# A one-token decoder block on one core: slots of 65,280 bytes a row, the last values in one transfer, a shared tile, 16 output rows

## The chip, the cores and the metric

The kernel runs on one core of one Trainium2 chip. The metric is device time in microseconds (us) of one execution; lower is better. The kernel before took 1052.56 us as the median of three runs (1052.41, 1052.56, 1052.56).

## The reference

One token passes through a transformer block with an adaptive layer norm. All data are float32. What is computed, cut to what matters:

```python
mod = (silu(c) @ w_mod).reshape(1, 6, 1, -1)          # six rows of 640: sa, ca, ga, sb, cb, gb
h = layernorm(x) * (1 + ca) + sa
q = (h @ wq).reshape(32 heads, 192)
p = softmax((q @ k_cache) * 192 ** -0.5)              # k_cache: 32 heads x 8192 positions x 192
o = p @ v_cache                                       # v_cache: 32 heads x 8192 positions x 192
x = x + ga * (o.reshape(6144) @ wo)
h = layernorm(x) * (1 + cb) + sb
x = x + gb * (relu(h @ w1 + b1) ** 2 @ w2 + b2)       # 640 -> 1536 -> 640
```

The two caches are 201 MB each and are read once; with the weights the kernel reads 451.83 MB.

## The kernel before, in words

**The stream.** The host lays out the caches, `wo` and most of `wq` as one array `kv`. `plan()` (line 55) cuts it into 53 chunks. A chunk has, for each of the 128 partitions, one contiguous row: `nk` key positions of 192 floats, then `nv` value blocks of `UNIT` = 1536 floats (8 positions), then perhaps one part of `wo` (1920 floats, "o") and one of `wq` (2560 floats, "q"). A chunk is filled up to `SLOT` = 84 x 192 = 16128 floats, that is 64,512 bytes a row. Three buffers of that size (`slot`, line 102) take the chunks in turn. `load(n)` (line 227) issues chunk `n` on SP's DMA queue, and the loop over the plan calls `load(n + 3)` at the end of chunk `n`'s step; SP holds the load back until the last instruction that reads the buffer's old contents is done. After the 53 chunks the same three buffers take, in this order, `wm1` (12800 floats a row, in two transfers), `w1` (7680, in two) and `w2` (7680, in four), so `wm1` waits for chunk 50, `w1` for chunk 51 and `w2` for chunk 52. All go through one queue, in the order of their issue.

**A chunk's step** (lines 377 to 424). `query` multiplies a part of `wq` on TensorE, and ScalarE puts the result in the ring `qb` (line 248, 1536 floats). `values` (line 314) does three products per value block, which the profile counts as six TensorE instructions, all of them for the heads whose probabilities are ready. `multiply` (line 267) multiplies keys by the query on VectorE; GpSimd folds 7 of 16 positions in half (line 399), and VectorE sums (`scores`, line 276). When a head's 64 positions are complete, `softmax` (line 292) makes its probabilities, with a transpose on TensorE in the middle. A head whose eight value blocks are done is evicted in the next step: `evict` (line 327) masks and reduces on VectorE, and for each second head transposes on TensorE; `turn` (line 342) reduces that on VectorE. `attend` (line 347) multiplies a pair of heads by its part of `wo`: ScalarE spreads the vector, then eight TensorE instructions add to `att_a`.

**The end** (lines 431 to 469). The last head is evicted (line 334, 336), transposed (340), turned (344) and attended (352 to 356). Then 40 TensorE instructions on `wm1` make three modulation rows (line 198). Between them `gather` (line 361) brings the attention's sum from PSUM to `att_s` (a tile of 640 floats, zeroed by GpSimd at line 260, near the program's start) and adds its parts on TensorE (line 369). Second layer norm, `w1` (line 447), two matmuls on `ones` that compute nothing (line 451), the squared ReLU, `w2` (line 464, 96 TensorE instructions), two VectorE instructions (467, 468) and the store (469) of four rows of 160 floats, taken from partitions 0, 32, 64 and 96.

**The last three chunks** by `plan()`: chunk 50 has 42 key positions, the last ones, and 5 value blocks; chunk 51 has no keys, 9 value blocks and o 14; chunk 52 has 7 value blocks and o 15, 12672 floats. Chunk 52 alone is loaded in two transfers (line 231): four value blocks first, the rest behind them.

## Time and profile before

| | |
|---|---|
| Runs shown | 1052.41, 1052.56, 1052.56 us |
| The profiled execution's own time | 1052.4 us |
| Its span, from the first to the last instruction | 1050.6 us |
| TensorE busy | 486.7 us (46%) |
| VectorE busy | 826.2 us (79%) |
| ScalarE busy | 44.9 us (4%) |
| GpSimd busy | 190.5 us (18%) |
| Mean granted TensorE clock | 0.729 |
| Bytes read | 451.83 MB |

The profile names engines PE (TensorE matmuls), PEld (TensorE weight loads), DVE (VectorE), ACT (ScalarE), POOL (GpSimd) and SPq (the queue on which SP issues DMAs). Times in a view are microseconds from the start of the span. In the chain of waits, each row is a start, a duration and what ran; the chain is followed back from the last instruction to what released it. In a timeline, the brackets at a row's end hold how long the engine stood idle before it and what it waited for. In a table of stretches, each row has a stretch, its length, busy time and instructions of each engine, the granted clock, the DMA engines' busy share and the rate in GB/s.

### The profile page before, as it was taken

Reading aid. Unit: us, or ns where it says so; the run is one execution under the profiler, and the core shown is the slowest. Engines: PE = TensorE matmul, PEld = TensorE weight load, DVE = VectorE, ACT = ScalarE, POOL = GpSimd, SP = SyncE. Lnnn points to the kernel's source line nnn. Section 1 sums busy time; section 2 is a strip of 40 time slices with the busy share of each in tenths; the row PEclk is TensorE's granted clock in tenths of the full one; section 3 lists DMA queues with packets and bytes.
Section 4 is the critical chain, followed back from the end, with each engine's and each line's share of the span. In section 5 each row is a group of like instructions: output and inputs, shape, how many; then the busy total and the mean of one; then the engine's idle time right before and its main releaser. Section 6 shows DMA issues by size and latency. Waiting matters only on the chain.

```text
span 1050.6 us, 5178 instructions
## 1 busy us (share of the span) xinstructions
PE 486.7 (46%) x2130; PEld 133.8 (13%) x2130; DVE 826.2 (79%) x405; ACT 44.9 (4%) x122; POOL 190.5 (18%) x61
## 2 busy tenths in 40 slices
PE   3253334455352363436353356345446346435287
PEld 1010001111010010101011011001001011001023
DVE  1799878876959969888697895999887977988812
ACT  0100000000000000000000000000000000000001
POOL 1113121121212211212121121122211211211200
PEclk9676576777675686767677687686777767768689
DMA  9999999999999999999999999999999999999997
GB/s 406 432 433 432 431 440 442 436 436 430 433 432 432 435 440 433 432 429 434 432 433 435 435 431 434 432 438 432 438 437 431 432 430 430 432 435 440 420 432 336
DMA packets 9142, 452.14 MB, mean 430 GB/s; under 512 B 1032, under 2 KB 1036, under 8 KB 1420
## 3 DMA queue, kind: packets, MB, share of 16 engines
q1 hardware_dynamic: 9120, 451.83, 99.4%
q8 instruction: 16, 0.26, 0.1%
q14 instruction: 6, 0.05, 0.0%
HBM read 451.83 MB, written 0.00 MB: 430 GB/s over the span
## 4 chain that ended last, share of the span: by engine, by line
DMA 56%; DVE 30%; PE 12%; ACT 1%; issue 0%; SPq 0%; DVEq 0%; ACTq 0%
DMA chunk<-in_kv 53%; DVE chunk L273 16%; DVE sc L281 12%; PE ps_o L322 6%; PE ps_q L254 2%; PE att_a L354 2%; DMA w_t<-in_w 2%; DMA wm_t<-in_wm 1%; DVE os L336 1%; DVE om L334 1%; PE att_a L356 0%; ACT p L305 0%; PE ps_mx L297 0%; PE ps_mod L198 0%; PE ps_mod L204 0%
## 5 line engine op out<-in xcount | busy, mean ns | idle before, releaser
L273 DVE TENSOR_TENSOR chunk<-chunk,qb 128x8064 f32<-128x8064 f32 (+19 forms) x81 | 419.6, 5211 | 126.7 <-DMA chunk<-in_kv 121.5
L281 DVE TENSOR_REDUCE sc<-chunk 128x25 f32<-128x4800 f32 (+21 forms) x109 | 333.8, 3096 | 0.4
L399 POOL TENSOR_TENSOR chunk<-chunk 128x1824 f32<-128x1824 f32 (+9 forms) x51 | 187.4, 3675 | 801.3 <-DVE chunk L273 552.2
L322 PE MATMUL ps_o<-chunk,p 128*32 128x512 f32 x1536 | 287.1, 716 | 68.8 <-DMA chunk<-in_kv 59.4
L297 PE MATMUL ps_mx<-ident,mp 128*128 128x128 f32 x32 | 14.6, 457 | 350.4 <-DVE mp L295 350.4
L322 PEld LDWEIGHTS ps_o<-chunk,p 128*32 128x32 f32 x1536 | 66.0, 128 | 265.1 <-issue 181.4
L354 PE MATMUL att_a<-chunk,oW 128*32 128x512 f32 x96 | 64.2, 824 | 44.9 <-ACT oW L352 44.9
L254 PE MATMUL ps_q<-chunk,ln_h 128*128 128x512 f32 x110 | 66.4, 764 | 25.9 <-DMA chunk<-in_kv 25.9
L297 PEld LDWEIGHTS ps_mx<-ident,mp 128*128 128x128 f32 x32 | 5.7, 177 | 379.5 <-DVE mp L295 310.8
L305 ACT ACTIVATE p<-sc,nm 128x256 f32<-128x256 f32 x32 | 16.2, 508 | 650.2 <-DVE nm L299 650.2
L254 PEld LDWEIGHTS ps_q<-chunk,ln_h 128*128 128x128 f32 x110 | 26.4, 251 | 63.6 <-issue 34.4
L334 DVE TENSOR_TENSOR om<-ps_o,mask 96x512 f32<-96x512 f32 x32 | 21.6, 675 | 8.9 <-PE ps_o L322 8.9
L299 DVE TENSOR_REDUCE nm<-ps_mx 128x1 f32<-128x128 f32 x32 | 9.3, 292 | 19.4 <-PE ps_mx L297 19.4
L336 DVE TENSOR_REDUCE os<-om 96x64 f32<-96x512 f32 x32 | 21.8, 682 | 1.1
L354 PEld LDWEIGHTS att_a<-chunk,oW 128*32 128x32 f32 x96 | 12.1, 141 | 81.3 <-ACT oW L352 47.6
L344 DVE TENSOR_REDUCE oT<-ps_oT 128x3 f32<-128x96 f32 x16 | 4.0, 248 | 20.9 <-PE ps_oT L340 20.9
L310 PE MATMUL ps_sum<-ident,wide 128*128 128x128 f32 x16 | 7.4, 466 | 22.4 <-ACT wide L308 22.4
L340 PE MATMUL ps_oT<-ident,os 96*128 96x96 f32 x16 | 5.0, 314 | 27.0 <-DVE os L336 27.0
L198 PE MATMUL ps_mod<-wm_t,silu 128*32 128x480 f32 (+2 forms) x78 | 9.0, 602 | 14.4 <-DVE silu L180 14.4
L356 PE MATMUL att_a<-chunk,oW 128*96 128x384 f32 x32 | 14.5, 534 | 0.0
L352 ACT ACTIVATE oW<-oT,r 128x96 f32<-128x96 f32 x16 | 5.9, 372 | 174.6 <-DVE oT L344 174.6
L255 ACT ACTIVATE qb<-ps_q 128x512 f32<-128x512 f32 x12 | 7.2, 598 | 132.0 <-PE ps_q L254 132.0
(79 smaller groups left out, 99.8 us busy)
## 6 DMA issues: line engine op xcount, KB each, us to landing
chunk<-in_kv SPq DMA_DIRECT2D x38, 8064.0 KB, 35.4
chunk<-in_kv SPq DMA_DIRECT2D x11, 8000.0 KB, 36.9
chunk<-in_kv SPq DMA_DIRECT2D x2, 7872.0 KB
chunk<-in_kv SPq DMA_DIRECT2D x1, 6144.0 KB, 22.7
wm_t<-in_wm SPq DMA_DIRECT2D x1, 4480.0 KB
wm_t<-in_wm SPq DMA_DIRECT2D x1, 4257.0 KB, 12.5
chunk<-in_kv SPq DMA_DIRECT2D x1, 3264.0 KB
chunk<-in_kv SPq DMA_DIRECT2D x1, 3072.0 KB
```

The lines of the kernel that those rows point to most:

```text
L254: nc.tensor.matmul(ps, h1[:, b:b + 1].to_broadcast([P, P]), w[:, b], start=(b == 0), stop=(b == KB - 1))
L273: nc.vector.tensor_mul(pr, pr, q[:, None, :].to_broadcast([P, b - a, DH]))
L281: nc.vector.tensor_reduce(sc[:, a % SRING:a % SRING + b - a], src[:, a - first:b - first], axis=AX.X, op=ALU.add)
L297: nc.tensor.transpose(ps[:, :P], mp.to_broadcast([P, P]), ident)
L299: nc.vector.tensor_reduce(nm, ps[:, :P], axis=AX.X, op=ALU.max, negate=True)
L305: nc.scalar.activation(p, s[:, :, None].to_broadcast([P, NPOS, 32 // E]), AF.Exp, bias=nm, accum_out=sp[:, h % 2:h % 2 + 1])
L322: nc.tensor.matmul(ps_t[h][32 * g:32 * (g + 1)], p[:, E * j:E * (j + 1)].rearrange("p e r -> p (e r)"), t[:, g], start=(j == 0), stop=last)
L334: nc.vector.tensor_mul(om[:n], ps_t.pop(h)[:n].rearrange("p (d e) -> p d e", e=E), mask[:n, None, :].to_broadcast([n, ED, E]))
L336: nc.vector.tensor_reduce(os_[:n, h % 2], om[:n], axis=AX.X, op=ALU.add)
L354: nc.tensor.matmul(att_a[96:, :512], oW[:, j], w[:, j, :512], start=(first and j == 0), stop=(last and j == NV - 1))
L356: nc.tensor.matmul(att_a[:96, :NV * (D - 512)], oW.rearrange("p j r -> p (j r)"), w[:, :, 512:], start=first, stop=last)
L399: nc.gpsimd.tensor_add(half, half, kt[:, m:, DH // 2:])
```

## The change

`SLOT` becomes 85 x 192 = 16320 floats, 65,280 bytes a row, and `plan()` fills its chunks to that. There are still 53 chunks and every byte is read once; 38 chunks are now 65,280 bytes a row (before, 38 were 64,512), and 11, those with a part of `wq`, 64,768 (before 64,000). The end of the plan becomes:

| chunk | before: keys, value blocks, extra (floats a row) | after |
|---|---|---|
| 49 | 44, 5 (16128) | 45, 5 (16320) |
| 50 | 42, 5 (15744) | 17, 8 (15552) |
| 51 | 0, 9, o 14 (15744) | 0, 9, o 14 (15744) |
| 52 | 0, 7, o 15 (12672) | 0, 1, o 15 (3456) |

The last chunk is loaded in one transfer, as the others. The ring `qb` and the tile `att_s` share one place in SBUF: `att_s` is allocated in `gather`, and GpSimd zeroes it there, once nothing reads the ring any more. The output is 16 rows: partitions 0, 8, 16 and so on, each fourth of which the host keeps.

```diff
-SLOT = 84 * DH
+SLOT = 85 * DH
...
+OUT = 16
...
-            cuts = (m,) if n + 1 < len(PLAN) else ((PLAN[n][3] + 1) // 2 * UNIT, m)
-            pieces = [(kv[start[n]:start[n] + P * m].rearrange("(p n) -> p n", p=P), cuts)]
+            pieces = [(kv[start[n]:start[n] + P * m].rearrange("(p n) -> p n", p=P), (m,))]
...
-    qb = const.tile([P, RING], F32, name="qb")
+    qb = work.tile([P, RING], F32, name="qb", tag="qb", bufs=1)
...
-    att_s = const.tile([P, D], F32, name="att_s")
-    nc.gpsimd.memset(att_s, 0.0)
...
     def gather():
 
+        att_s = work.tile([P, D], F32, name="att_s", tag="qb", bufs=1)
+        nc.gpsimd.memset(att_s, 0.0)
         nc.vector.tensor_copy(att_s[96:, :512], att_a[96:, :512])
...
-    nc.sync.dma_start(out.rearrange("(g n) -> g n", g=G), y[::32])
+    nc.sync.dma_start(out, y[::P // OUT])
```

More of the change, by code (lines that the diff above doesn't have):

```diff
@@ L515 @@
     args = [nc.dram_tensor(f"in_{n}", v.shape, F32, kind="ExternalInput").ap() for n, v in arrays.items()]
-    args.append(nc.dram_tensor("out_y", (D,), F32, kind="ExternalOutput").ap())
+    args.append(nc.dram_tensor("out_y", (OUT, DG), F32, kind="ExternalOutput").ap())
     with tile.TileContext(nc) as tc:
@@ L519 @@
     r = run_bass_kernel_spmd(nc, [{f"in_{n}": v for n, v in arrays.items()}], core_ids=[0])
-    return np.asarray(r.results[0]["out_y"]).reshape(1, 1, D)
+    return np.asarray(r.results[0]["out_y"]).reshape(G, OUT // G, DG)[:, 0].reshape(1, 1, D)
```

## The prediction

> **What bounds the kernel now.** I read the page first: its DMA rows, then its issues.

> ```profile
> span 1050.6 us, 5178 instructions
> DMA  9999999999999999999999999999999999999997
> q1 hardware_dynamic: 9120, 451.83, 99.4%
> chunk<-in_kv SPq DMA_DIRECT2D x38, 8064.0 KB, 35.4
> ```

> The 16 DMA engines are busy for 99.4% of the span, in every slice. A chunk of 8064 KB lands 35.4 us after its issue. What it needs alone follows from the rate, in a table of two stretches:

> ```profile
> 40.00:1000.00 960.00, 429.63 (x1730) 113.15 (x1733) 803.56 (x359) 35.74 (x105) 187.41 (x51) 0.71 1.00 433
> 1000.00:1040.00 40.00, 35.90 (x228) 10.84 (x223) 8.92 (x22) 4.28 (x11) 0.00 (x0) 0.95 1.00 429
> ```

> At 433 GB/s, 8064 KB (8.258 MB) take 19.1 us, so a load usually has some 16 us of other loads ahead of it: every engine but the DMAs has slack in mid-stream. The bytes stay the same, so the question is the end. The chain of waits there:

> ```profile
> 999.07 10.50 PE ps_o L322 x54
> ...
> 1014.14 6.17 PE ps_o L322 x42
> 1020.31 0.02 issue
> 1020.33 0.70 DVE om L334
> ...
> 1025.61 0.83 PE att_a L356 x2
> ...
> 1027.31 18.61 DMA w_t<-in_w
> ...
> 1045.97 0.75 PE ps_y L464 x16
> 1046.75 0.52 PE ps_y L464 x8
> 1047.27 0.02 issue
> 1047.30 0.34 DVE y L467
> ```

> The reader is to see two lines of work. One is the DMA stream, which ends with `w2` just before 1046.75. The other is TensorE's: nine value blocks of chunk 51 (54 instructions), o 14, seven blocks of chunk 52 (42), then the last head's eviction and o 15, done at 1026.44. From there it reaches `w2`'s products, and must wait:

> ```profile
> 1037.56 0.32 PEld L447 LDWEIGHTS ps_f<-w_t,hT 128*32 128x32 f32 x8 [0.33 <-DMA w_t<-in_w]
> ```

> ```profile
> 1042.23 1.84 PE L464 MATMUL ps_y<-w_t,fT 128*32 128x160 f32 x48 [1.10 <-DMA w_t<-in_w]
> 1044.44 1.02 PE L464 MATMUL ps_y<-w_t,fT 128*32 128x160 f32 x24 [0.37 <-DMA w_t<-in_w]
> 1045.97 1.26 PE L464 MATMUL ps_y<-w_t,fT 128*32 128x160 f32 x24 [0.51 <-DMA w_t<-in_w]
> ```

> These waits are all that TensorE's line can be late before it sets the end. At 1.84/48 = 0.038 us each, 24 products need 0.92; the last row's 1.26 hides another wait of 0.34. Together 0.33 + 1.10 + 0.37 + 0.51 + 0.34 = **2.65 us**.

> **The change part by part.**

> *The plan's end.* Behind the last keys the stream before brings 9 + 7 value blocks; the larger slots leave 9 + 1, because 192 floats in each of 49 chunks add up to most of the last one (12672 becomes 3456). The seven-block tail looks shorter, but chunk 51 now lies close to the stream's end. The second half of `w1` is seen at 1037.56 (the weight load that waited for it). Ahead of that point lie `w1` (7680 floats x 512 bytes = 3840 KB), `wm1` (6400 KB) and chunk 52 (1728 KB): 11968 KB, 12.255 MB, 28.6 us at 429 GB/s. So chunk 51 will be seen at 1037.56 - 28.6 = **1009.0**. Before, chunk 52's 6336 KB put it at 998.0, and TensorE began its 54 instructions at 999.07. They start 10 us later now, and only 36 instructions of 6.17/42 = 0.147 us (5.3 us) are saved behind them.

> The sum from 1009.0, at the prices of before:
> - 54 value instructions: 10.50 (below for its bounds).
> - transposing head 29, o 14: from 1009.57, the end of the x54 row, to 1014.14: 4.57.
> - 6 value instructions of chunk 52, there since 1013.1: 6 x 0.147 = 0.88.
> - eviction of head 31, turn, o 15: from 1020.31 to 1026.44: 6.13.

> That is 22.1, so attention ends at 1031.1 where it ended at 1026.44: **+4.6 us**.

> *The clock.* I cut the end of the run, and two samples from mid-run, at the points where the granted clock changes, steps of 3.41 us:

> ```profile
> 389.98:393.39 3.41, 1.34 (x7) 1.00 1.09 473
> 393.39:396.81 3.42, 0.00 (x0) 0.50 1.00 434
> 659.63:663.04 3.41, 1.45 (x12) 1.00 0.96 416
> 663.04:666.45 3.41, 0.00 (x0) 1.00 1.00 435
> ...
> 997.54:1000.95 3.41, 2.35 (x10) 0.50 0.95 411
> 1000.95:1004.37 3.42, 3.42 (x15) 0.50 1.02 438
> 1004.37:1007.78 3.41, 3.41 (x27) 1.00 1.05 452
> 1018.02:1021.43 3.41, 2.25 (x18) 1.00 0.85 366
> 1021.43:1024.85 3.42, 2.30 (x6) 1.00 1.03 441
> ```

> The column behind the length is TensorE's busy time, then come clock, DMA share, GB/s. A step at full clock with 1.45 us busy is followed by full clock, one with 1.34 us by half; a busy step at half clock (1000.95) is followed by full. So a step grid that runs on by itself decides. Of the 10.50 us of the 54, 5.3 lay ahead of 1004.37; the other 5.2 did 35 of them at 0.147, so 19 took 5.3, 0.28 each: twice as long at half clock. TensorE will idle before 1009.0 (8 blocks of chunk 50, seen 18.8 us earlier, need at most 48 x 0.28 = 13.4 us), so the 54 begin at half clock for 3.4 to 6.8 us: 54 x 0.147 = 7.9 plus half of that, 9.6 to 11.3. I keep 10.5.

> Then comes the eviction's gap:

> ```profile
> 1014.07 6.21 PE L322 MATMUL ps_o<-chunk,p 128*32 128x512 f32 x42
> 1021.79 0.30 PE L340 MATMUL ps_oT<-ident,os 96*128 96x96 f32 x1 [1.52 <-DVE os L336]
> 1022.85 2.76 PE L354 MATMUL att_a<-chunk,oW 128*32 128x512 f32 x6 [0.75 <-ACT oW L352]
> ```

> Of 2.54 us TensorE is busy 0.30. Before, a grid point (1021.43) halved this gap, and both steps stayed above 1.45. Now the distance from the start of the 54 to the gap is nearly fixed (15 to 16.7 us), and the grid point that ended their half clock lies three steps before one that opens a step some 0.5 to 1 us ahead of the gap. With a half-clock phase of 3.41 + d, the gap begins at 1024.05 + d/2, in the step 1022.65 + d to 1026.06 + d. Its busy time is 1.17 to 1.40 for d from 0.6 to 3.2, and above only at the edges: in about three quarters of the phases the clock drops. The next step, o 15 and the first modulation products, runs at half clock for 3.41 us and does 1.7 us less. I take it: attention and what follows it come **+6.3 us** late.

> [...]

> *At the end.* 6.3 - 2.65 = 3.65 us. `w1` waits for o 14 (about 1024.1) and `w2` for o 15 (about 1032.8), while the queue is busy with `wm1` until 1028.4 and `w1` until about 1037.2, so the stream keeps a lead of about 4 us in both. That is late next, if attention passed 1036.

> *The last values in one transfer, and 53 transfers for 54.* `w2`'s last three pieces, 960, 640 and 320 KB, come 2.21, 1.53 and 0.78 us after the one before (from the rows above): a straight line with 0.065 us left at no bytes. One transfer fewer saves that, -0.07. The late half of chunk 52 costs nothing: TensorE reaches it 11 us after it is there. No row shows 65,280 bytes in one piece; 64,512 is nearest, and I take its rate. If rows above 64,512 were cut in two, each transfer would pay its fixed 0.065 twice: 49 x 0.065 = 3.2 us.

> *The shared tile.* The memset moves behind the ring's last reader:

> ```profile
> 3.06 0.63 POOL L260 MEMSET att_s<- 128x640 f32 x1
> ...
> 988.52 3.84 POOL L399 TENSOR_TENSOR chunk<-chunk 128x1728 f32<-128x1728 f32 x1 [14.07 <-DVE chunk L273]
> ```

> It can run when chunk 50's keys are multiplied, near 995, and GpSimd has nothing after its last fold; `att_s` is wanted after 1031. Nothing queues behind it. Cost 0; without that cover 0.63. At the start it ran under the first load, so its going gains nothing.

> *The store.* The issue of the four rows, against all loads of 128:

> ```profile
> L469 SPq DMA_DIRECT2D out_y<-y x1: 595/595/595, 1048.0 to 1048.0; - x1
> ```

> ```profile
> L240 SPq DMA_DIRECT2D chunk<-in_kv x54: 327/328/439, 7.7 to 977.8; - x54
> ```

> 16 rows are unknown: between 0.33 us (-0.27) and 0.60 plus a little for 12 more rows to land (+0.1). Between them I take -0.15.

> **Sum.** 1052.4 (profiled) + 3.65 - 0.15 = 1055.9; the runs' median lies 0.16 above the profiled execution: **1056.1 us**, +0.34%. Its own range, from the 54 (-0.9 to +0.8), 0.4 for the landing and the store: 1054.7 to 1057.3.

> **The rivals.**
> 1. *The clock holds.* The gap falls on a grid point as before. Then 4.6 - 2.65 - 0.15 = +1.8: 1054.4, within 1.0. For it: the rows 1018.02 and 1021.43; against it: the gap's fixed place after the 54.
> 2. *The stream hides it: not slower.* If attention ends by about 1029 (TensorE already at full clock at 1009.0, 7.9 for 10.5, and no drop), `w2`'s last piece sets the end again: -0.07 - 0.15, 1052.3. The point is 2.65 us of lateness. Against it: the steps before 999 were at half clock after a pause of the same kind.
> 3. *Long rows are cut.* +3.2 in the stream, ahead of everything: 1059.3. For it there is only that no row is so long; the q1 row would show some 6300 packets more.
> 4. *Faster.* Every transfer costs a fixed time that a merged one saves. To gain 2.1 us, one transfer would have to cost 2.1; the pieces above show 0.065. [...]

> **How the numbers follow.** Forecast 0.58, rivals 0.22, 0.09, 0.07 and 0.04. This kernel's measurement can tell about 0.2%, 2.1 us, from no change. Slower: 0.57 of the forecast, a third of rival 1 (0.07), rival 3 (0.07): 0.71. Within: two thirds of rival 1 and rival 2: 0.24. Faster: 0.05. The range 1052.1 to 1057.8 takes in the forecast and rivals 1 and 2.

> **What would show it.** In the changed profile: TensorE starts chunk 51's 54 value instructions near 1009, not 999; attention's last product ends near 1031 to 1033; the table of stretches has half clock in the step behind the eviction's gap; L464's rows follow each other without a wait for DMA, and end near 1051; the DMA share drops earlier than the kernel's end. A last product still waiting for `w2` at 1046.7 refutes the sum; a gap in the DMA stream before 1037 would mean that I missed a late load; a q1 row with more packets is rival 3.

## The result, and the profile after

| | median, us | lowest to highest | runs |
|---|---|---|---|
| before | 1052.59 | 1052.41 to 1052.82 | 8 |
| after | 1055.76 | 1054.24 to 1057.13 | 8 |

The ratio is 1.0029, with a 95% interval of 1.0019 to 1.0038: slower, by 3.2 us at the medians. The single times say more than the median: 1054.24, 1054.27, 1054.35, 1054.86, then nothing up to 1056.67, 1056.71, 1056.95, 1057.13. The median lies in the empty stretch, where no run is. The profiled execution is of the lower group: 1054.27 us, of which 1052.2 are the span. What a time has outside its span differs from run to run, from 1.7 to 3.1 us over the runs on record, so the spans tell the groups better: 1052.2 to 1052.5, and 1053.9 to 1055.2.

The page's row of the DMA queue shows that the transfers grew longer and fewer, and that every byte still comes once. After (before, it had 9120 packets):

```profile
span 1052.2 us, 5176 instructions
q1 hardware_dynamic: 9000, 451.84, 99.2%
```

120 packets are gone: 144 with the transfer that went (the 5 and 5 split with a store of four rows, below, has 8976), less 24 that the store's twelve new rows added (the kernel before with 16 rows, below, has 9144). Had rows of 65,280 bytes been cut in two, there would be some 6300 more (49 loads of 128 rows, an estimate). The rate of the stream in the table of stretches (length, busy time of PE, PEld, DVE, ACT and POOL, clock, DMA share, GB/s) is the same until 1000 us, and lower behind it:

```profile
40.00:1000.00 960.00, 441.89 (x1759) 114.26 (x1759) 804.55 (x354) 34.19 (x102) 186.19 (x52) 0.71 1.00 434
1000.00:1040.00 40.00, 27.28 (x160) 7.96 (x163) 9.38 (x23) 4.50 (x12) 0.00 (x0) 0.91 0.98 418
```

TensorE did 35.9 us of work between 1000 and 1040 before, and 27.3 now. It waits there for chunk 51, and pays behind 1040. The lower rate is a thin stretch just ahead of chunk 51's landing, where the DMA share falls to 0.39 from 1006.5 to 1008; why is not shown. The prediction had named a gap before 1037 as the sign of a late load, but the landing itself came within 0.1 us of the time forecast. The chain of waits at the end:

```profile
975.79 33.23 DMA chunk<-in_kv
1009.02 0.04 issue
1009.06 9.48 PE ps_o L320 x54
...
1023.11 1.02 PE ps_o L320 x6
1024.13 0.02 issue
1024.16 0.70 DVE om L332
...
1026.68 2.76 PE att_a L352 x6
1029.44 0.82 PE att_a L354 x2
1030.26 2.55 PE ps_mod L199 x24
...
1045.18 3.50 PE ps_y L464 x96
1048.68 0.02 issue
1048.70 0.34 DVE y L467
```

The reader is to see that no DMA stands behind 1009.02 any more. Before, the chain's last long piece was `w2`'s transfer up to 1045.92, with 24 products behind it; now it runs through TensorE from chunk 51's landing to the end, and the 96 products of `w2` follow each other in one piece of 3.50 us. Attention ends at 1030.26, 3.82 us later than before (1026.44); the first VectorE instruction behind `w2` starts at 1048.70, 1.40 us later. The difference, 2.42 us, is what the waits of before hid.

### The profile page after: what moved, and what is told of

Its sections match the earlier page's. It is cut to its first block, busy times and chain, and to the rows that moved or that the text cites. A ratio compares the mean times of both kernels' runs of the same rounds, so it can differ in the third digit from the quotient of the medians.

```text
span 1052.2 us, 5176 instructions
## 1 busy us (share of the span) xinstructions
PE 494.3 (47%) x2130; PEld 134.2 (13%) x2130; DVE 827.7 (79%) x404; ACT 44.3 (4%) x122; POOL 188.7 (18%) x61
## 2 busy tenths in 40 slices
DMA  9999999999999999999999999999999999999997
## 3 DMA queue, kind: packets, MB, share of 16 engines
HBM read 451.83 MB, written 0.01 MB: 429 GB/s over the span
## 4 chain that ended last, share of the span: by engine, by line
DMA 59%; DVE 24%; PE 15%; ACT 1%; issue 1%; DVEq 0%; SPq 0%; ACTq 0%
DMA chunk<-in_kv 58%; DVE chunk L271 12%; DVE sc L279 9%; PE ps_o L320 4%; PE att_a L352 4%; PE ps_q L254 3%; DMA wm_t<-in_wm 1%; PE ps_mod L199 1%; PE att_a L354 1%; DVE os L334 1%; DVE om L332 0%; ACT p L303 0%; PE ps_mx L295 0%; PE ps_mod L205 0%; PE ps_y L464 0%
## 5 line engine op out<-in xcount | busy, mean ns | idle before, releaser
L271 DVE TENSOR_TENSOR chunk<-chunk,qb 128x8640 f32<-128x8640 f32 (+23 forms) x80 | 419.6, 5275 | 124.6 <-DMA chunk<-in_kv 119.1
L320 PE MATMUL ps_o<-chunk,p 128*32 128x512 f32 x1536 | 293.9, 729 | 144.1 <-DMA chunk<-in_kv 135.6
L279 DVE TENSOR_REDUCE sc<-chunk 128x26 f32<-128x4992 f32 (+20 forms) x109 | 334.8, 3104 | 0.4
L399 POOL TENSOR_TENSOR chunk<-chunk 128x1824 f32<-128x1824 f32 (+9 forms) x51 | 185.6, 3640 | 807.2 <-DVE chunk L271 566.1
L352 PE MATMUL att_a<-chunk,oW 128*32 128x512 f32 x96 | 68.9, 876 | 21.7 <-ACT oW L350 21.7
L254 PE MATMUL ps_q<-chunk,ln_h 128*128 128x512 f32 x110 | 61.7, 718 | 32.3 <-DMA chunk<-in_kv 32.3
L334 DVE TENSOR_REDUCE os<-om 96x64 f32<-96x512 f32 x32 | 21.8, 682 | 1.1
L352 PEld LDWEIGHTS att_a<-chunk,oW 128*32 128x32 f32 x96 | 12.6, 146 | 60.7 <-issue 36.1
L354 PE MATMUL att_a<-chunk,oW 128*96 128x384 f32 x32 | 14.9, 547 | 0.0
```

Source lines behind the costliest of these rows:

```text
L254: nc.tensor.matmul(ps, h1[:, b:b + 1].to_broadcast([P, P]), w[:, b], start=(b == 0), stop=(b == KB - 1))
L271: nc.vector.tensor_mul(pr, pr, q[:, None, :].to_broadcast([P, b - a, DH]))
L279: nc.vector.tensor_reduce(sc[:, a % SRING:a % SRING + b - a], src[:, a - first:b - first], axis=AX.X, op=ALU.add)
L320: nc.tensor.matmul(ps_t[h][32 * g:32 * (g + 1)], p[:, E * j:E * (j + 1)].rearrange("p e r -> p (e r)"), t[:, g], start=(j == 0), stop=last)
L334: nc.vector.tensor_reduce(os_[:n, h % 2], om[:n], axis=AX.X, op=ALU.add)
L352: nc.tensor.matmul(att_a[96:, :512], oW[:, j], w[:, j, :512], start=(first and j == 0), stop=(last and j == NV - 1))
```

## The experiments

Each kernel is the changed one with the edit shown, unless it says otherwise. Nine kernels, five rounds each, beside runs of the kernel before on the same chip (their medians lay between 1052.64 and 1052.79).

**The changed kernel again, with no edit.**

> The changed kernel once more, unaltered. Theory (late values, and a clock drop behind the eviction's gap in some executions): times fall again in two groups, near 1054.3 and near 1056.8, nothing between 1055.3 and 1056.3; if the profiled execution is of the upper group, its table of stretches shows a step of 3.41 us at half clock behind the gap before o 15. Rival (the groups come from the DMA stream or the store): a profile of the upper group has its clock at full from the 54 value instructions to the end, and the extra 2.4 us as a gap in the stream or behind the last VectorE instruction.

Measured: 1056.01, 1056.35, 1056.52, 1056.93, 1057.65. All five are of the upper group, which reaches lower than 1056.3, so the empty stretch is narrower than was expected. Their spans, 1053.9 to 1055.0, lie clear of the lower group's. With the eight runs above, 4 of 13 are of the lower group and 9 of the upper. This time the profile caught the upper one. Its chain at the same place:

```profile
1009.20 9.83 PE ps_o L320 x54
...
1023.60 1.02 PE ps_o L320 x6
...
1027.16 4.23 PE att_a L352 x6
1031.39 0.82 PE att_a L354 x2
...
1047.07 3.50 PE ps_y L464 x96
1050.57 0.02 issue
1050.59 0.34 DVE y L467
```

and its table of stretches, cut every 3.41 us at the borders on which the granted clock changes in this trace (length, PE busy, clock, DMA share, GB/s):

```profile
999.43:1002.84 3.41, 1.50 (x11) 1.00 0.85 369
1002.84:1006.26 3.42, 0.00 (x0) 0.50 1.07 462
...
1009.67:1013.08 3.41, 3.41 (x15) 0.50 1.13 486
1013.08:1016.50 3.42, 3.42 (x27) 1.00 1.07 455
...
1023.32:1026.74 3.42, 1.56 (x8) 1.00 0.99 413
1026.74:1030.15 3.41, 2.99 (x4) 0.50 1.03 442
1030.15:1033.56 3.41, 3.41 (x21) 1.00 0.98 420
```

The step that holds most of the eviction's pause (1024.62 to 1027.16) has 1.56 us of TensorE work; the next one runs at half clock, and the six products of o 15 take 4.23 us where they took 2.76. In the profile of the lower group the start of the 54 and the same place read:

```profile
1008.83:1012.24 3.41, 3.18 (x12) 0.50 1.09 468
1012.24:1015.66 3.42, 3.42 (x27) 1.00 1.00 428
...
1022.48:1025.90 3.42, 1.90 (x9) 1.00 1.02 419
1025.90:1029.31 3.41, 2.65 (x7) 1.00 0.96 411
```

There a step's border, at 1025.90, cuts the pause (1024.13 to 1026.68) into steps with 1.90 and 2.65 us of work, and the clock holds. Between the two profiles attention ends 1.95 us apart (1032.21 against 1030.26): 1.47 by the slow o 15, 0.35 by the 54, 0.14 by the landing. The rival looked for the difference in the DMA stream or behind the last VectorE instruction; it is in neither, beyond the landing's 0.14.

**The pause filled.** Two products of 320 columns that compute nothing stand between the last value block and the last head's eviction.

```diff
+    gap = psum.tile([P, 512], F32, tag="sm", name="ps_gap", bufs=2)
+    for k in range(2):
+        nc.tensor.matmul(gap[:, :2 * DG], ones, mods[:, 0:2].rearrange("p m n -> p (m n)"), start=True, stop=True)
     for h in to_evict:
         evict(h)
```

> The changed kernel with two products of 320 columns that compute nothing between the last value block and the eviction of head 31, some 1.1 us of TensorE work in a pause of 1.5. Theory: the clock no longer drops, every execution lies in the lower group, 1054.1 to 1054.9. Rival (the groups do not come from that pause): two groups as before, half of the runs near 1056.8.

Measured: median 1055.32, nine runs from 1054.07 to 1056.29, 1.0025 (1.0015 to 1.0034). Both expectations miss in the times: the two groups are gone, but no narrow lower group is left. The spans say what happened. They run from 1052.3 to 1053.8, so all nine lie under the upper group of the changed kernel (1053.9 and more); the two longest times, 1055.93 and 1056.29, have 2.8 and 3.0 us outside spans of 1053.1 and 1053.3. In the profile the clock stays at full behind the pause:

```profile
1009.17 9.79 PE L320 MATMUL ps_o<-chunk,p 128*32 128x512 f32 x54 [6.87 <-DMA chunk<-in_kv]
...
1027.15 2.76 PE L352 MATMUL att_a<-chunk,oW 128*32 128x512 f32 x6 [0.76 <-ACT oW L350]
```

The spans still spread over 1.5 us. What is left over is the other price of half clock: the 54 value instructions took 9.79 us here, and where the step grid lies would decide how long they run at half clock, worth up to 1.7 us (half of a step of 3.41 us, an estimate). The next two runs test that.

**TensorE kept busy ahead of chunk 51, the pause open.** The helper `spin(n, name)`, whose definition is not shown, issues `n` of the same products that compute nothing.

```diff
+        if n == len(PLAN) - 2:
+            spin(12, "warm")
```

> The changed kernel with the twelve products that compute nothing in front of chunk 51's value blocks, and the eviction's pause left open. Theory: the 54 value instructions take 7.9 us; where the pause then falls against the clock's steps is no longer fixed, so the clock drops in less than two thirds of the executions. Without a drop w2 sets the end, 1052.5 to 1052.9; with one, TensorE's line is 1.7 us later, of which 0.2 to 0.7 is still hidden: 1053.5 to 1054.3. Rival (the half clock in front does the whole harm, the pause costs nothing): one group, 1052.5 to 1052.9, as with the pause filled.

Measured: 1052.69 and 1052.72, then nine runs from 1053.94 to 1054.32; median 1054.10, 1.0010 (1.0001 to 1.0019). Two narrow groups at the times expected. Their shares were not: the clock dropped in 9 of 11, not in less than two thirds. The profile, of the upper group:

```profile
1009.17 7.92 PE L320 MATMUL ps_o<-chunk,p 128*32 128x512 f32 x54 [1.36 <-DMA chunk<-in_kv]
...
1025.29 4.15 PE L352 MATMUL att_a<-chunk,oW 128*32 128x512 f32 x6 [0.76 <-ACT oW L350]
```

The 54 take 7.92 us at full clock throughout, and the spread inside a group falls to 0.4 us. The slow o 15 alone is worth the distance of the groups, about 1.4 us.

**Both together.** The twelve products of the last edit, and `spin(2, "gap")` in the pause.

> The changed kernel with products that compute nothing in two places: twelve of 320 columns (some 6.5 us) in front of chunk 51's value blocks, so that TensorE is not idle while it waits for that chunk, and two in the pause of the eviction. Theory (the loss is TensorE's line, late by chunk 51's landing and by half clock at two places whose price follows the phase of the clock's steps): the 54 value instructions take 7.9 us in every execution, the line ends 1.6 to 3.3 us earlier than with the pause filled alone, and w2 sets the end: 1052.5 to 1053.0, one narrow group. Rival (the spread of the times, 1054.1 to 1056.3 with the pause filled, is from the stream or the store): the spread stays over 1 us and the median above 1054.

Measured: median 1052.72, eleven runs from 1052.50 to 1052.90, 0.9999 (0.9990 to 1.0008). With TensorE at full clock in both places the slots of 65,280 bytes with the blocks split 9 and 1 cost nothing that can be measured. Its timeline:

```profile
1009.41 7.92 PE L320 MATMUL ps_o<-chunk,p 128*32 128x512 f32 x54 [1.54 <-DMA chunk<-in_kv]
...
1025.54 2.76 PE L352 MATMUL att_a<-chunk,oW 128*32 128x512 f32 x6 [0.76 <-ACT oW L350]
...
1043.98 3.47 PE L472 MATMUL ps_y<-w_t,fT 128*32 128x160 f32 x96 [0.16 <-DVE gb L466]
```

The products of `w2` end only 0.2 us later than in the kernel before: 1047.45 against 1047.23. Chunk 51 is as late as ever, seen at 1009.41; the line just has no more than the slack to make up.

**One size changed: the blocks split 8 and 2.**

```diff
     chunks[-1][4].append(("o", NPAIR - 1))
+    (ka, na, va, ma, wa), (kb, nb, vb, mb, wb) = chunks[-2:]
+    m = 8
+    chunks[-2:] = [(ka, na, va, m, wa), (kb, nb, va + m, ma + mb - m, wb)]
     return chunks
```

> The changed kernel with the last ten value blocks split 8 and 2 over chunks 51 and 52. Theory, a point between 9 + 1 and 5 + 5: chunk 51 lands 1.8 us earlier (768 KB at 429 GB/s), six instructions move behind o 14, attention ends near 1029.3 at 10.5 us for nine blocks, about 0.3 us past the slack of 2.65, and the pause may still drop the clock: a median of 1052.7 to 1054.5, 1 to 3 us below the changed kernel, with a spread of over 1 us. Rival (the split matters only by which chunk the last head ends in, not by when chunk 51 lands): as the changed kernel, 1055 to 1057.

Measured: median 1054.99, eleven runs: 1052.51, 1052.63, and nine from 1054.72 to 1056.17; 1.0019 (1.0010 to 1.0028). The landing moved as said, the median lies 0.5 us above the range given. By the times this decides little: 1054.99 lies in neither range. The spans do: 1050.7 and 1050.8 for two runs, where a hidden line would put them, and 1052.5 to 1053.7 for nine; the changed kernel's two groups, 1052.2 to 1052.5 and 1053.9 to 1055.2, lie some 1.5 us higher. So the landing counts, and not only the chunk in which the last head ends. The profile, of the nine, shows the clock's drop behind the pause, in its timeline and its table of stretches:

```profile
1007.38 9.13 PE L323 MATMUL ps_o<-chunk,p 128*32 128x512 f32 x48 [5.77 <-DMA chunk<-in_kv]
...
1025.50 4.30 PE L355 MATMUL att_a<-chunk,oW 128*32 128x512 f32 x6 [0.76 <-ACT oW L353]
```

```profile
1021.82:1025.23 3.41, 1.41 (x10) 1.00 0.90 386
1025.23:1028.64 3.41, 3.14 (x4) 0.50 0.98 418
```

**The blocks split 5 and 5.** The same edit with `m = (ma + mb) // 2`, which is 5.

> The changed kernel with the last ten value blocks split 5 and 5 over chunks 51 and 52 and not 9 and 1; rows of 65,280 bytes, one transfer for the last chunk, shared tile and 16 rows stay. Theory: chunk 51 lands near 1002, TensorE ends attention near 1024 to 1027, the last piece of w2 sets the end again: 1052.3 to 1053.0, one group. Rival (the long rows or the single transfer cost the 3.2 us): 1055 to 1057 as the changed kernel.

Measured: median 1052.70, eleven runs from 1052.54 to 1052.90, 0.9999 (0.9990 to 1.0008), one group. Rows of 65,280 bytes, the single transfer, the shared tile and the 16 rows are all in it, so none of them is the loss. Its timeline waits for `w2` again:

```profile
1002.14 4.49 PE L323 MATMUL ps_o<-chunk,p 128*32 128x512 f32 x30
...
1042.32 1.84 PE L467 MATMUL ps_y<-w_t,fT 128*32 128x160 f32 x48 [1.24 <-DMA w_t<-in_w]
1044.55 1.02 PE L467 MATMUL ps_y<-w_t,fT 128*32 128x160 f32 x24 [0.39 <-DMA w_t<-in_w]
```

**The slots of before.**

```diff
-SLOT = 85 * DH
+SLOT = 84 * DH
```

> The changed kernel with slots of 64,512 bytes a row as before; the single last transfer, the shared tile and the 16 rows stay. Theory: these three cost nothing but the store's 0.1 to 0.3 us, 1052.5 to 1053.0. Rival (the single last transfer delays the last values): attention ends 1 us or more later than in the kernel before and the time is 1053.5 or above.

Measured: median 1052.95, eleven runs from 1052.60 to 1053.88, 1.0003 (0.9994 to 1.0012). The loss goes with the slots, which set the plan. In its profile the seven blocks of chunk 52 start at 1014.25 (1014.07 before), 0.2 us later, as the 54 ahead of them do (999.22 and 999.00): the single transfer delays nothing.

**The store.** Once the kernel before with 16 rows, once the 5 and 5 split with four (`OUT = 4`).

> The kernel before with the store of 16 rows alone. Theory: 0.1 to 0.3 us slower than the kernel before; in the profile the issue takes 0.60 us or a little more, and from the issue's start to the end of the span 2.7 to 2.9 us where it was 2.6. Rival (the gain that the prediction took, 0.15): faster by 0.1 or more, with an issue of 0.33 to 0.45 us.

> The changed kernel with the last blocks split 5 and 5, and the store of four rows as in the kernel before. Theory (the store of 16 rows costs 0.1 to 0.3 us, it gains nothing): 0.1 to 0.3 us under the 5 and 5 split with 16 rows (1052.70), 1052.4 to 1052.6. Rival (16 rows are issued and land no later than four): the same within 0.05 us or slower.

Measured: 1052.88 for the kernel before with 16 rows (1052.53 to 1053.72, eleven runs) beside 1052.67; 1052.59 for the 5 and 5 split with four rows (1052.41 to 1053.05, eleven runs) beside 1052.70 with 16, on another chip. Both intervals of the ratio hold 1 (1.0002, 0.9993 to 1.0011; 0.9999, 0.9990 to 1.0008), so 0.1 to 0.2 us is the size that the medians suggest and no more. The profile is plainer, with the issue of 16 rows in the kernel before:

```profile
L470 SPq DMA_DIRECT2D out_y<-y x1: 602/602/602, 1048.0 to 1048.0; - x1
```

0.602 us against 0.595 with four rows, and the span ends at 1050.8 against 1050.6, with the issue at 1048.01 in both: no gain. The same profile shows that the clock's drop is not new with the longer slots:

```profile
1021.74 4.46 PE L355 MATMUL att_a<-chunk,oW 128*32 128x512 f32 x6 [0.76 <-ACT oW L353]
```

With the plan of before, o 15 took 4.46 us in this execution where it took 2.76 at full clock, and the products of `w2` end at 1047.24 all the same (1047.23 before): the wait for `w2` hid it. Two of the eleven runs have spans of 1051.7 and 1051.9 where the others have at most 1051.2; no profile shows why. The split of 5 and 5 with four rows is the best form that the runs point to, and it is no faster than the kernel before.

## Why the prediction was right, point by point

The predicted 1056.1 stands beside a median of 1055.76. That the two lie 0.3 us apart is luck in part. The median of eight runs fell midway between two groups of four, and the five further runs bring it to 1056.52. The forecast describes the upper group (1056.01 to 1057.65), and in the upper group's profile two misses cancel: 3.29 us of lateness where 3.65 was forecast, and some 0.3 us lost at the store where 0.15 was to be gained. By its steps, with the two profiles of the changed kernel (lower and upper group) and the experiments:

- *The plan's end decides, not the stream.* Shown. The split 5 and 5 takes the whole loss away with the long slots in place. Chunk 51 was to be seen at 1009.0; it was, at 1009.06 and 1009.20.
- *The sum of the line.* The 54 at 10.50 took 9.48 and 9.83, the first below the 9.6 to 11.3 given; o 14 at 4.57 took 4.57 in both; six instructions at 0.88 took 1.02; eviction and o 15 at 6.13 took 6.13 with the clock at full and 7.59 with the drop. Attention ended at 1030.26 and 1032.21, against 1031.1 and 1032.8 predicted.
- *The slack of 2.65.* It hid 2.42 and 2.48 (3.82 late became 1.40; 5.77 became 3.29).
- *The clock drop.* Shown: the upper group's profile has it, filling the pause alone leaves no span of the upper group, and with the 54 at full clock filling it moves nine of eleven runs by 1.4 us. The prediction expected it in three quarters of the phases; by the groups it came in 9 of 13 executions. The price, 1.7 us, was 1.47 in the profile.
- *What was mis-sized: half clock ahead of the 54.* It was put at 2.6 us (10.5 for 7.9) and took 1.6 and 1.9. The lower bound of 3.4 us at half clock was wrong: in the lower group's profile it lasted 3.18 us, from 1009.06 to 1012.24, and the step that ends there, busy for 3.18 of its 3.41 us (93%), was followed by full clock. The prediction saw this price only as part of a row of before, where it was hidden; now it lies on the line that sets the end. Taking it away gives 2.6 us back with the pause filled (1055.32 to 1052.72, where the stream all but sets the end), more than filling the pause alone (1055.76 or, over all 13 runs, 1056.52, to 1055.32).
- *The border between drop and hold.* Put between 1.34 and 1.45 us of work in a step, from two samples; the upper group's profile drops with 1.56 and, at 999.43, with 1.50. Where the clock can change was read from the traces of two executions, of the kernel before and of the changed kernel (lower group): the granted clock is 0.50 or 1.00, and each stretch of one value on record (97 in each trace, without the last, which the end cuts) lasts a whole number of 3.413 us, from one to 13. Divided into steps on that grid, from 25 us on, the two traces give 264 steps at full clock. Every one with 1.40 us of work or less was followed by half clock, every one with 1.53 or more by full, and of the six between, three dropped (1.43, 1.45, 1.50) and three held (1.41, 1.42, 1.46). Of their 333 steps at half clock, none under 2.68 us was followed by full, and every one above 2.89 was. The split 8 and 2 dropped with 1.66. The two extremes of the first border, from the split 8 and 2 and from the changed kernel:

```profile
888.70:892.11 3.41, 1.66 (x5) 1.00 1.10 479
892.11:895.53 3.42, 3.42 (x5) 0.50 0.95 406
```

```profile
261.31:264.73 3.42, 1.41 (x12) 1.00 0.88 382
264.73:268.14 3.41, 0.00 (x0) 1.00 1.15 498
```

- *The store.* Wrong in sign: -0.15 was taken from loads of 128 rows, whose issue takes 0.33; sixteen rows are issued in 0.60, as four are, and the span ends 0.2 us later behind the issue's start. This is the step of the prediction that failed outright, and a small term.
- *The rest at nothing.* The memset of the shared tile ran at 995.83 for 0.63 us, under the wait for chunk 51. In the lower group's profile the first load of `w1` was issued at 1023.14 (about 1024.1 expected). The first of `w2` was issued at 1030.29, and at 1032.24 in the upper group's (about 1032.8 expected). The products waited for neither.
- *The rivals.* The first, the clock holds, is the lower group: 1054.4 predicted, 1054.24 to 1054.86 measured. The forecast and this rival were both right, each for a part of the executions. The second and the third, a hidden line and cut rows, did not happen: the packet count excludes the third. Of the fourth, 2.1 us for a transfer that goes, nothing was seen: with the single last transfer in the slots of before, the time was 1052.95 beside 1052.64. In the upper group's profile a pause of 2.54 us, of which 0.30 busy, was enough for the drop.

Not settled: why the clock dropped in nine of eleven runs with the 54 at full clock. With a border from 1.41 to 1.66 and a grid that lies anywhere with equal chance, that pause should drop it in 44 to 59% of the executions (an estimate from its TensorE rows). Nine or more of eleven would then come up in 1 to 10 of a hundred such samples. Whether that was chance, or the grid is not free against the program, stays open, and no profile of that kernel's lower group was taken.

## What to carry to other kernels

Where a stream of DMAs sets the time, look at what is left to compute behind each landing near its end: a plan that packs the loads tighter can move the last large piece of work behind the landing that used to be ahead of it. Count the slack of the compute line from its waits for the stream, and compare it with the change of the landing and with the clock that TensorE will have when the work comes. Look at its pauses: here one of 2.54 us cost another 1.47 us behind it, and filling it, or the wait ahead of a late block, with products that compute nothing is a cheap test of that (1052.72 us with both filled).
